# Six small loads for two, in a decode kernel bound by its transfers

## The chip, the cores and the metric

The kernel runs on one core of a Trainium2 chip. The metric is the device time of one execution, in microseconds; the median of several runs counts. The profile shows one execution, with times counted from the start of its span.

## The reference

The result is `x + attention(xn) + gMLP(xn)`, with `xn` the layer norm of `x`, for one decode step: four batch rows of 640 numbers, in bf16.

```python
# attention: 32 heads of 128, 4096 cached positions per batch row and head
q = (xn @ wq) -> [B, 32, 1, 128]
scores = einsum('bhqd,bhkd->bhqk', q, k_cache) * 128 ** -0.5
o = einsum('bhqk,bhkd->bhqd', softmax(scores), v_cache)
attention = o.reshape(B, 1, 4096) @ wo
# gMLP: w_in [640, 1728], w_out [864, 640]; the sequence has length 1
z = gelu(xn @ w_in);  z1, z2 = z[..., :864], layernorm(z[..., 864:])
gMLP = (z1 * (w_sp * z2 + b_sp)) @ w_out
```

The two caches are 134 MB each and every number of them is used once, so the work is mostly the reading of 282 MB.

## The kernel before

The caches are read in 16 runs (`NT`), one for each group of eight heads and each batch row: 8.4 MB of K and 8.4 MB of V per run. All of K, V and the early weights pass through one large SBUF tile, `ring`, which is cut into five units; K takes two units at a time and V one or two. For each quarter of a K run, DVE multiplies by the query (L555), often adds the halves (L575), PE sums (L584) and DVE finishes the row sums (L598). The softmax follows on DVE, ACT and PE, and PE multiplies the dealt-out probabilities with V (L657). At the end of a head group the output projection adds into `out_ps` (L755).

All loads but three tiny ones are issued by SyncE (SP), in an order written out by hand: a list `loads` of planned transfers, from which `pump()` sends the next one once the units that it overwrites were used. The first entries are: wq (L110, sent before the list), the first K run in two halves (L153), the gMLP's weights (`load_w`), the second K run (L153, one transfer of 8.4 MB), the first part of wo (L172), and the first run's V in two halves (L161). The second K run overwrites wq, so it must also wait for the last matmul of L357. The second V half overwrites the gMLP's weights, and so waits for the gMLP's last matmul (L516). ACT issues x (L96) and two scalars (L114, L115) at the very start.

`load_w` sends `w_in` (L133, 2160 KB), the first 768 rows of `w_out` (L134, 960 KB), and the last 96 rows of `w_out` in two transfers of 60 KB (L141). These 96 rows go to 16 + 16 partitions, three rows (`TR`) of 640 numbers to each, dealt so that neighbouring partitions hold rows from four different places (`NW`); a memset on GpSimd (L138) zeroes the partitions around them first.

The framework gives the transfers issued by SP and ACT eight semaphores, numbered 0 to 7, in turn, in the order of the program. A transfer that takes a semaphore again first waits, in its issuer's queue, until the transfer that had it before, eight earlier, has landed. In the order of the program the first eight are x (0), wq (1), the two scalars (2 and 3), the two halves of the first K run (4 and 5), `w_in` (6) and the large part of `w_out` (7). The two transfers of L141 then take 0 and 1, the second K run 2, wo 3, and so on. The last two of the program are the stores of the result: half of it from SP (L849), half from ACT (L851), on semaphores 2 and 3.

The program ends (L877) with five wait instructions on SP, each for two semaphores, a drain, and two barriers of all engines. The five wait for semaphores 3 and 2, 4 and 1, 5 and 0, then 6 and DVE, 7 and ACT, in this order.

Of the kernel before, what the change touches and what calls it, by code (L numbers as in the profile page):

```python
# [20 lines left out]
def kernel(  # L21
# [14 lines left out]
    nc = tc.nc  # L36
    P = nc.NUM_PARTITIONS
    Bsz, Sq, D = A_x.shape
# [20 lines left out]
    CW = 32  # L59
# [4 lines left out]
    NFF = Fh // P  # L64
    NW = 4
    TL = P // CG // 2
    TR = (Fh - NFF * P) // (2 * TL)
# [57 lines left out]
    w_out_sb = w_sb[:, DC * F : DC * F + NFC * D].rearrange("p (k n) -> p k n", k=NFC)  # L125
# [6 lines left out]
    def load_w():  # L132
        nc.sync.dma_start(out=w_in_sb, in_=B_w_in.rearrange("(p c) n -> p c n", c=DC))  # L133
        nc.sync.dma_start(  # L134
            out=w_out_sb[:, 0:NFF, :],
            in_=B_w_out[0 : NFF * P].rearrange("(p k) n -> p k n", k=NFF),
        )
        nc.gpsimd.memset(w_out_sb[:TN, NFF:, :], 0.0)  # L138
        for g in range(2):
            at = NFF * P + g * TL * TR  # L140
            nc.sync.dma_start(  # L141
                out=w_out_sb[g * CW : g * CW + TL, NFF:, :].rearrange("p r n -> p (r n)"),
                in_=B_w_out[at : at + TL * TR].rearrange("(k e r) n -> e k (r n)", e=NW, r=TR),
            )

    k_tiles, v_tiles = {}, {}
    V_CUTS = (0, UC // 2, 3 * UC // 4, 7 * UC // 8, UC)
# [45 lines left out]

    plan_k(0)
    plan("w", W_UNIT, 1, load_w)
    plan_k(1)
    plan_wo(0)
# [20 lines left out]
    def pump():  # L218
        while loads:
# [29 lines left out]
        out=lane_diag[:],  # L249
        in_=ident_f[:].rearrange("p (h l) -> p l h", h=HT),  # L250
# [5 lines left out]
        out=hmask[:],  # L256
        in_=ident_f[:].rearrange("p (h l) -> p h l", h=HT),
# [5 lines left out]
        out=head_scale[:].rearrange("p (h l) -> p h l", h=HT),  # L263
# [11 lines left out]
        out=sel[:],  # L275
        in_=ident_f[:].rearrange("p (g h k) -> p k h g", g=CG, k=GC),
# [5 lines left out]
        out=spread[:],  # L282
        in_=ident[:].rearrange("p (m r) -> p r m", r=HT)[:, :, None, :].to_broadcast(
            [P, HT, HT, LN]
        ),
# [3 lines left out]
        out=q_lanes[:].rearrange("r b (h l) -> r b h l", h=HT),  # L289
        in_=ident[: HT * Bsz, : HT * Bsz]  # L290
# [9 lines left out]
    for g in range(CG):  # L300
        ps = slice(g * QW, (g + 1) * QW)
        for hh in range(QH):
            at_col = (g % 2 * QH + hh) * Bsz
            nc.gpsimd.tensor_copy(
                out=place[ps, hh, at_col : at_col + Bsz], in_=lane_diag[ps, 0:Bsz]
# [13 lines left out]
    for i in range(NSTAT):  # L319
# [5 lines left out]
        out=rstd[:], in_=mv[:, 1:2], func=ACT.Sqrt, bias=eps_tile[:Bsz], scale=1.0  # L325
# [4 lines left out]
        out=xn_bf[:],  # L330
# [9 lines left out]
    for c in range(DC):  # L340
        nc.tensor.transpose(  # L341
            out=xnT_ps[:, c, :], in_=xn_v[:, c, :], identity=ident[:Bsz, :Bsz]
# [11 lines left out]
    for c in range(DC):  # L354
        for hg in range(NQG):
            g = hg % CG
            nc.tensor.matmul(  # L357
                out=q_ps[hg // CG][g * QW : (g + 1) * QW, :],
# [11 lines left out]
    def out_sum(half):  # L370
        return out_ps[OG * half : OG * half + Bsz, :]

    for half in range(2):
        nc.tensor.matmul(
            out=out_sum(half),
# [390 lines left out]
    with tc.manual_schedule(engines={E.PE, E.DVE, E.Activation, E.SP}):  # L766
# [80 lines left out]
        r0, r1 = slice(0, Bsz), slice(OG, OG + Bsz)  # L847
# [34 lines left out]
```

## Time and profile before

| | |
|---|---|
| median of three runs | 661.8 us (661.74 to 661.94) |
| the profiled execution: time, span | 661.8 us, 660.0 us |
| busy: PE, DVE, ACT | 324.5, 463.6, 84.9 us |
| DMA read, mean rate over the span | 282.24 MB, 428 GB/s |
| granted TensorE clock | 0.717 |
| chain that ended last: DMA, DVE, PE | 63%, 29%, 6% |
| landing of ACT's store, SP's last drain starts, end of span | 658.93, 659.26, 660.0 us |

The span covers the engines' instructions; 1.8 us of the execution lie around it. The chain is followed back from the last instruction: at each step to whatever released it. A transfer's landing is the last of the semaphore writes of the DMA engines that carry it, and "us to landing" counts from the start of its issue on the queue of SP or ACT. Beside the page and its views, the text uses the trace's single DMA packets (start, duration, size) and the single semaphore writes.

### The profile page before, as it was taken

To read this page: it belongs to the slowest core of one execution; us is meant where nothing else is said; L and a number is where in the kernel's file an instruction comes from. 1 tells how busy PE (TensorE), PEld (TensorE's weight loads), DVE (VectorE), ACT (ScalarE), POOL (GpSimd) and SP (SyncE) were. 2 spreads that over 40 slices of the span, in tenths; PEclk is the share of its full clock that TensorE was granted. 3 is DMA by queue.
4 is the path that set the end of the run, shared out by engine and by line. 5 is a ranking of instruction groups with operands and counts; after the bars stand their busy time and mean duration, and the time that the engine had idled before them with its cause. 6 is when DMAs were issued, how large, how long until landed. Compare 5 with 4: busy or idle time off the path is not lost.

```text
span 660.0 us, 4943 instructions
## 1 busy us (share of the span) xinstructions
PE 324.5 (49%) x2127; PEld 147.6 (22%) x2127; DVE 463.6 (70%) x268; ACT 84.9 (13%) x208; POOL 8.6 (1%) x31
## 2 busy tenths in 40 slices
PE   0257463625636463464625346253564525347756
PEld 0114131211312221131212123011231212213333
DVE  2497966939598694957949297692957849498840
ACT  0023011020200202020020200202020020201100
POOL 4000000000000000000000000000000000000000
PEclk9767585775857577686768878567786768887786
DMA  9999999999999999999999999999999999999997
GB/s 380 433 449 406 440 447 433 442 418 441 438 425 437 442 425 426 433 442 437 437 442 405 438 441 433 442 425 438 425 437 442 437 429 438 417 426 437 424 429 289
DMA packets 7977, 282.56 MB, mean 428 GB/s; under 512 B 872, under 2 KB 2036, under 8 KB 2452
## 3 DMA queue, kind: packets, MB, share of 16 engines
q1 hardware_dynamic: 7936, 282.24, 99.1%
q8 instruction: 16, 0.26, 0.1%
q14 instruction: 5, 0.04, 0.0%
q10 hardware_dynamic: 20, 0.01, 0.0%
HBM read 282.24 MB, written 0.01 MB: 428 GB/s over the span
## 4 chain that ended last, share of the span: by engine, by line
DMA 63%; DVE 29%; PE 6%; issue 1%; ACT 0%; SPq 0%; DVEq 0%
DMA ring<-in_A_k_cache_dram 53%; DVE ring L555 20%; DMA ring<-in_A_v_cache_dram 9%; DVE halved L575 5%; PE s_ps L584 3%; DVE ring L575 3%; PE pv_acc L657 1%; PE zT L416 1%; DVE s_sb L598 0%; PE out_ps L755 0%; ACT L471 0%; PE pv L675 0%; SPq L161 0%; PE pv L687 0%; DVE o_r L743 0%
## 5 line engine op out<-in xcount | busy, mean ns | idle before, releaser
L555 DVE TENSOR_TENSOR ring<-ring,qbc 128x8192 bf16<-128x8192 bf16 x64 | 282.0, 4418 | 90.5 <-DMA ring<-in_A_k_cache_dram 90.5
L584 PE MATMUL s_ps<-ring,ident 128*128 128x512 bf16 x480 | 169.0, 521 | 259.6 <-DVE ring L575 152.2
L584 PEld LDWEIGHTS <-ident 128*128 128x128 bf16 x608 | 73.6, 121 | 409.6 <-issue 289.5
L575 DVE TENSOR_TENSOR ring<-ring 128x4096 bf16<-128x4096 bf16 x36 | 82.5, 2291 | 1.2
L657 PE MATMUL pv_acc<-ring,pm 128*32 128x512 bf16 x1008 | 73.0, 433 | 6.1 <-DMA ring<-in_A_v_cache_dram 6.1
L598 DVE TENSOR_REDUCE s_sb<-s_ps 128x64 f32<-128x512 f32 x64 | 43.9, 685 | 24.1 <-PE s_ps L584 24.0
L671 ACT COPY pv_sb<-pv_acc 128x512 f32<-128x512 f32 x16 | 9.4, 586 | 392.1 <-PE pv_acc L657 392.1
L584 PE MATMUL s_ps<-halved,ident 128*128 128x512 bf16 x128 | 39.9, 468 | 31.2 <-DVE halved L575 31.2
L632 ACT ACTIVATE pm<-p,hmask 128x256 bf16<-128x256 bf16 x120 | 49.5, 494 | 0.5
L657 PEld LDWEIGHTS <-pm 128*32 128x32 bf16 x1008 | 39.4, 145 | 41.1 <-issue 31.6
L575 DVE TENSOR_TENSOR halved<-ring 128x4096 bf16<-128x4096 bf16 x16 | 36.6, 2290 | 0.5
L617 DVE TENSOR_REDUCE nb<-max_ps 128x1 f32<-128x16 f32 x16 | 2.8, 174 | 38.1 <-PE max_ps L611 38.1
L675 PE MATMUL pv<-sel,pv_sb 128*128 128x8 f32 x128 | 17.0, 259 | 11.2 <-ACT pv_sb L671 11.2
L675 PEld LDWEIGHTS pv<-sel,pv_sb 128*128 128x128 f32 x128 | 15.5, 191 | 18.8 <-ACT pv_sb L671 18.8
L716 DVE TENSOR_TENSOR o_n<-pv,rden 128x32 bf16<-128x32 f32 x4 | 0.8, 191 | 14.4 <-PE pv L687 14.3
L609 ACT ACTIVATE lay<-lane_diag,m 128x16 f32<-128x16 f32 x16 | 4.9, 309 | 45.6 <-DVE m L607 45.6
L621 ACT ACTIVATE p<-s_sb,nb 128x256 bf16<-128x256 f32 x16 | 8.1, 508 | 20.6 <-DVE nb L617 20.6
L699 POOL TENSOR_TENSOR own_sum<-acc,hmask 128x32 f32<-128x32 f32 x4 | 2.0, 500 | 618.0 <-ACT p L621 618.0
L541 ACT CAST q_rows<-qr_ps 32x128 bf16<-32x128 f32 x4 | 1.0, 255 | 55.2 <-PE qr_ps L533 55.2
L611 PE MATMUL max_ps<-lay,head_scale 128*128 128x16 f32 x32 | 6.1, 265 | 3.1 <-ACT lay L609 3.1
L607 DVE TENSOR_REDUCE m<-s_sb 128x1 f32<-128x256 f32 x16 | 6.7, 420 | 0.5
L341 PE MATMUL xnT_ps<-ident,xn_bf 4*128 4x4 bf16 x5 | 0.4, 178 | 11.6 <-DVE xn_bf L329 11.6
(96 smaller groups left out, 88.4 us busy)
## 6 DMA issues: line engine op xcount, KB each, us to landing
ring<-in_A_v_cache_dram SPq DMA_DIRECT2D x7, 4096.0 KB, 21.9
ring<-in_A_k_cache_dram SPq DMA_DIRECT2D x2, 4096.0 KB, 29.2
ring<-in_A_wq_dram SPq DMA_DIRECT2D x1, 5120.0 KB
wo<-in_A_wo_dram SPq DMA_DIRECT2D x3, 1280.0 KB, 17.1
ring<-in_B_w_in_dram SPq DMA_DIRECT2D x1, 2160.0 KB, 38.5
ring<-in_A_v_cache_dram SPq DMA_DIRECT2D x1, 2048.0 KB, 20.5
ring<-in_A_v_cache_dram SPq DMA_DIRECT2D x1, 1024.0 KB
ring<-in_A_v_cache_dram SPq DMA_DIRECT2D x2, 512.0 KB
```

The costliest lines, as they stand in the source:

```text
L416: nc.tensor.matmul(out=zT[: P if k < NFF else TN, t, k, :], lhsT=w_t[:, 2 * c + t, k, :] if k < NFF else w_edge[:, 2 * c + t, k - NFF, :], ...
L555: nc.vector.tensor_tensor(out=t, in0=t, in1=qbcs[i // Bsz][:, i % Bsz, None, :].to_broadcast([P, QC, Dh]), op=ALU.mult,)
L575: nc.vector.tensor_tensor(out=h[:, :, 0:HD2], in0=t[:, :, 0:HD2], in1=t[:, :, HD2:Dh], op=ALU.add)
L584: nc.tensor.matmul(out=s[:], lhsT=ident[:], rhs=t[:, :, g * RW : (g + 1) * RW], start=(g == 0), stop=(g == n - 1),)
L598: nc.vector.tensor_reduce(out=scores[i][:, q * QC : (q + 1) * QC], in_=sums_ps.pop((i, q))[:], axis=AX.X, op=ALU.add,)
L607: nc.vector.tensor_reduce(out=m1[:], in_=scores[i][:], axis=AX.X, op=ALU.max)
L611: nc.tensor.matmul(out=ps[:], lhsT=head_scale[:], rhs=d[:], start=True, stop=True)
L621: nc.scalar.activation(out=p[:], in_=scores.pop(i)[:], func=ACT.Exp, bias=nb[:], scale=scale_qk, accum_out=acc[hg % NACC][:, b : b + 1],)
L632: nc.scalar.activation(out=p_m[i % 2][:, :, h, :], in_=probs[i][:].rearrange("p (n c) -> p n c", c=BC), func=ACT.Copy, scale=hmask[:, h : ...
L657: nc.tensor.matmul(out=pv_acc[g * CW : (g + 1) * CW, :], lhsT=pm[:, n, :, :].rearrange("p h (k c) -> p c (h k)", k=GC)[:, c, :], rhs=v_nat ...
L671: nc.scalar.copy(out=pv_sb[:], in_=pv_acc[:])
L675: nc.tensor.matmul(out=pvs[hg][:, :, b], lhsT=pv_sb[:, k * Dh : (k + 1) * Dh], rhs=sel[:, k, :], start=(k == 0), stop=stop and k == GC - 1,)
```

## The change

The first of the two small transfers becomes four, of four partitions each (every fourth partition of the 16, one contiguous 3,840-byte run to each). The second becomes two, by columns: the first two of the three rows of each partition, then the third. The bytes, their places and the zeroing are the same. Since six transfers stand where two stood, every later transfer takes a semaphore four further on: the second K run takes 6, wo 7, and the stores of the result 6 and 7. In the changed file all later lines move down by six: L153 becomes L159, L161 L167, L172 L178, L849 L855, L851 L857 and L877 L883.

```diff
         for g in range(2):
             at = NFF * P + g * TL * TR
-            nc.sync.dma_start(
-                out=w_out_sb[g * CW : g * CW + TL, NFF:, :].rearrange("p r n -> p (r n)"),
-                in_=B_w_out[at : at + TL * TR].rearrange("(k e r) n -> e k (r n)", e=NW, r=TR),
-            )
+            src = B_w_out[at : at + TL * TR].rearrange("(k e r) n -> e k (r n)", e=NW, r=TR)
+            dst = w_out_sb[:, NFF:, :].rearrange("p r n -> p (r n)")
+            lanes = slice(g * CW, g * CW + TL)
+            if g == 0:
+                for k in range(TL // NW):
+                    nc.sync.dma_start(out=dst[g * CW + k : g * CW + TL : NW], in_=src[:, k])
+            else:
+                for r0, r1 in ((0, TR - 1), (TR - 1, TR)):
+                    cs = slice(r0 * D, r1 * D)
+                    nc.sync.dma_start(out=dst[lanes, cs], in_=src[:, :, cs])
```

## The prediction

> **What bounds the kernel now.** I read the page first (engine shares, the 40 slices, the DMA queues), then the chain that ended last, then SP's timeline at the start, the rows of the lines that issue the weights, and last the trace's single DMA packets.
>
> From the page:
>
> ```profile
> PE 324.5 (49%) x2127; PEld 147.6 (22%) x2127; DVE 463.6 (70%) x268; ACT 84.9 (13%) x208; POOL 8.6 (1%) x31
> DMA  9999999999999999999999999999999999999997
> ...
> q1 hardware_dynamic: 7936, 282.24, 99.1%
> q8 instruction: 16, 0.26, 0.1%
> ```
>
> Queue q1 (everything that SP issues) keeps the 16 DMA engines busy for 99.1% of the span; no compute engine passes 70%. The kernel is bound by its transfers, so a microsecond in which DMA engines stand still is lost for good, and a late compute step costs nothing while transfers are queued. The chain of waits, around the second K run:
>
> ```profile
> 74.19 2.30 DVE halved L575
> 76.51 0.04 issue
> 76.55 28.43 DMA ring<-in_A_k_cache_dram
> ```
>
> The chain passes through DVE and SP's issue, but this load of 8.39 MB takes 28.4 us where its bytes need 19.3 at the packets' pace (below): it stands some 9 us behind earlier transfers. DVE or SP may come that much later before an engine runs dry. SP's own timeline at the start:
>
> ```profile
> 1.18 0.94 SPq L153 DMA_DIRECT2D ring<-in_A_k_cache_dram  x2
> 2.15 0.98 SPq L133 DMA_DIRECT2D ring<-in_B_w_in_dram  x1
> 3.17 0.53 SPq L134 DMA_DIRECT2D ring<-in_B_w_out_dram  x1
> 3.82 12.95 SPq L141 DMA_DIRECT2D ring<-in_B_w_out_dram  x2
> 20.27 0.34 SPq L153 DMA_DIRECT2D ring<-in_A_k_cache_dram  x1
> 20.65 0.42 SPq L172 DMA_DIRECT2D wo<-in_A_wo_dram  x1
> 39.34 26.87 SPq L161 DMA_DIRECT2D ring<-in_A_v_cache_dram  x2
> ```
>
> The second K run goes out at 20.27, released by L357's last matmul, 20 us before the engines reach it. The packets show the rest: each DMA engine works off its share in the order of issue, back to back (65,536 bytes every 2.415 us). On eleven engines the second K run's first packet starts at 41.48 to 41.92, straight behind w_out's last; on five, held up by L141 or a late start, at 42.56 to 42.97. Eight of the eleven are each interrupted twice by the page's 16 "instruction" packets (q8, 16 KB of code each), at 1.42 us a time: the packet itself 0.88 to 0.99, and the next K or V packet 2.89 to 2.97 instead of 2.42 (the excess is smaller on packets of half that size). These eight, whose second K run began at 41.48 to 41.79, are with one other the last to end: their last wo pieces land at 656.4 to 656.7, the other seven engines' at 653.9 to 655.7. The end is set by those eight.
>
> **The change, part by part.** The profiled execution took 661.8 us, 660.0 of them span, and 661.8 is also the median of the runs, so sums on its span apply to the median as they stand.
>
> *The tail.* SP ends with five wait instructions for two semaphores each and a drain:
>
> ```profile
> L877 SPq EVENT_SEMAPHORE  x7: 17/28/28, 658.9 to 659.9; - x7
> ```
>
> The first two-semaphore wait holds the stores' two (2 and 3). It passes at 658.944, after ACT's store lands at 658.93; four waits on things long done follow at 659.009, .070, .134 and .196, the drain at .261. With the stores on 6 and 7, three of the waits pass while the stores fly, the fourth at SP's store (landed 658.75), the fifth at 658.944, and the drain comes at about 659.01. Four steps of 0.063 go: **-0.25 us**. Nothing stands against it: the barriers behind the drain wait for SP.
>
> *The bytes.* On the engines, each L141 is 4 packets of 3,840 bytes, 149 ns each, on four engines. After: four transfers of one such packet on four engines, then the second group in packets of 2,560 and 1,280, by bytes some 99 and 50 ns. Per engine 8 x 149 = 1.19 us stays, plus four more closing semaphore packets of 9 ns: +0.04. The four engines are not among the eight; the nearest one ends 0.28 us before the last. Cost nothing; without that cover, 0.04. The Trainium skill, "DMA: Bandwidth & Descriptors", Rules for kernel authors, speaks against the split: coalesce small transfers, since under 64 KB one mostly pays overhead; here the second L141 lands 0.60 us behind the first on each engine, which is its 4 x 149 ns and no fixed part, so the trace does not agree for transfers queued behind others.
>
> *SP's issues.* L141 takes SP 0.80 and 0.64. Four more, at most 3.2 us, fall between 16 and 36 while SP has nothing else to send. PE's matmuls with the last weights must wait for six semaphores instead of two, at some 0.06 each 0.25 us later; behind them is L161's second V half (65.88), which stands behind queued work until 73.5. Nothing.
>
> *Who waits for whom at the start.* A DMA waits until the one eight issues before it, on the same semaphore, has landed. The six small ones now follow x, wq, the two scalars and the first K run's halves, which land by 35.5. But the second K run's predecessor moves from a scalar (landed 7.8) to **w_in**, and the wo load's from the other scalar to w_out. After these the spacing is eight as before, so only the names change. w_in lands late:
>
> ```profile
> L133 SPq DMA_DIRECT2D ring<-in_B_w_in_dram x1: 976/976/976, 2.2 to 2.2; - x1
> ...
> DMA to landing us min/median/max: 38.5/38.5/38.5
> ```
>
> 2.155 + 38.5 = 40.62, by its slowest engine (the others' shares land at 39.4 to 40.0). So the second K run is issued at 40.62 + 0.08 (a semaphore wait and the step behind it on SP) = 40.70 instead of 20.27. Behind it in SP's queue are wo (w_out lands 42.9) and the first V half, 39.34 before, about 43.4 after; both have the second K run's 19.3 us of packets as cover. Nothing for these two.
>
> *From issue to first packet.* No transfer of before is issued to engines about to run dry, except the very first: L110, issued at 0.734, has its first packets at 1.74 to 1.90 on twelve engines (1.01 to 1.16 later), on the other four at 2.08 to 2.80. So the second K run starts at 41.71 to 41.86. Engines that were to begin at 41.48 to 41.68 run dry. A stream that restarts is slow in its first packet: after a code load by 0.47 to 0.55 us, in L110's by 0.64 to 1.19 on most engines. I take 0.5, from the code load, since it is the row on a running machine with packets of this size. The eight engines then run as if begun at about 42.3, where the last of them had begun at 41.79: **+0.5 us** at the end. Bounds: none lost, if packets come at once; or L110's slowest engine, whose first packet ended at 5.20, as if begun at 3.68, 2.95 after issue: 40.70 + 2.95 - 41.79 = +1.9. The Trainium skill has in the same page, Latency and other measured facts, about 600 ns to the first byte of a DMA issued by SP; by that the packets would come at 41.30 and nothing would run dry, which is the first rival.
>
> Sum: 661.8 - 0.25 + 0.5 = **662.0 us**. K's own later landing (62.97 before; DVE takes it at 63.06) pushes DVE by the same half microsecond and then the next K issue from 76.55, covered by 9 us.
>
> **The rivals.**
> - *No gap*: the packets come before 41.48. For it: SP's 0.38 us of issuing is part of the 1.01 I counted, and the first transfer was cold. Against: the two stores at the end take 0.83 and 0.88 from issue to first packet too. It leaves the tail: 661.55. Chance 0.2.
> - *A cold restart, slower than before*: eleven engines restart together, as in L110, and one of the eight starts like L110's slowest: +1.9 - 0.25 = 663.4. For it: the only start from nothing in this trace. Against: that was one engine of sixteen. It is slower by over 0.2% once an engine of the eight counts as begun after 41.79 + 1.3 + 0.25 = 43.35. Chance 0.13; restarts between, at 662.4 to 662.9, are my forecast's upper side.
> - *A fixed cost per small transfer on its engines*, as large as SP's 0.80 for issuing: 4 x 0.80 - 0.28 - 0.25 = +2.7, 664.5. The 0.60 between the two L141 speaks against. Chance 0.02.
> - *The change does not do what it says*: the stores sit on other semaphores. The built program has them on 6 and 7; left out. Faster by over 0.2% needs more than the whole tail step; one code load less on each of the eight would spare 1.42 and give 660.1, but the change leaves PE's code as long as it was. Chance 0.03 for it and the like.
>
> **How the numbers follow.** The forecast, 661.8 to 662.9 with the restart at about half a microsecond, has 0.62. A measurement of this kernel tells about 0.2%, 1.3 us, from no change: forecast and first rival lie within, so same 0.82; slower 0.15 from the second and third; faster 0.03. The range takes in the first rival and most of the way to the second: 661.4 to 663.1.
>
> **What would show it.** In the profile after: SP's second K issue (L159) at 40.7 and wo behind 42.9; DMA packets of the second K run starting at 41.7 to 41.9 with first packets near 2.9 us; the last wo landing 0.5 later against the span's start; SP's last drain 0.07 after the store's landing instead of 0.32. Wrong, if L159 goes out near 20, if the first packets join w_out's without a gap, or if the eight engines no longer end last.

## The result, and the profile after

| | before | after |
|---|---|---|
| median of the runs side by side, us | 661.96 (661.74 to 662.16) | 663.78 (663.16 to 664.40) |
| ratio | | 1.0027, 95% interval 1.0017 to 1.0036 |
| profiled execution: time, span, us | 661.8, 660.0 | 663.82, 662.0 |
| second K run issued | 20.27 | 40.73 |
| second K run landed | 62.97 | 65.46 |
| last wo piece landed | 656.67 | 658.66 |
| ACT's half of the result cast | 657.17 | 659.30 |
| last store landed, SP's last drain | 658.93, 659.26 | 661.12, 661.26 |

The change costs 1.8 us; 662.0 was forecast. The page of after, for the same lines as before:

```profile
PE 319.6 (48%) x2127; PEld 148.8 (22%) x2127; DVE 463.5 (70%) x268; ACT 84.9 (13%) x208; POOL 8.7 (1%) x31
...
DMA  9999999999999999999999999999999999999997
GB/s 376 434 400 421 438 439 432 444 432 440 433 424 428 444 436 437 424 433 440 436 425 440 437 424 440 429 440 441 420 436 437 432 436 437 432 411 438 437 419 280
...
q1 hardware_dynamic: 7968, 282.25, 99.0%
q8 instruction: 16, 0.26, 0.1%
```

The same rates line on the page of before:

```profile
GB/s 380 433 449 406 440 447 433 442 418 441 438 425 437 442 425 426 433 442 437 437 442 405 438 441 433 442 425 438 425 437 442 437 429 438 417 426 437 424 429 289
```

The busy shares tell nothing: a DMA engine counts as busy while a slow packet runs. The rates do. By the end of the fourth slice before has moved (380 + 433 + 449 + 406) x 16.50 us = 27.5 MB, after (376 + 434 + 400 + 421) x 16.55 us = 27.0 MB in 0.2 us more: 0.62 MB short, 1.4 us at 428 GB/s (roughly, since the line counts a whole packet in the slice where it starts). The loss arises in the third slice, 33 to 50 us: 400 where before has 449. The chain there:

```profile
2.65 38.01 DMA ring<-in_B_w_in_dram
40.66 0.02 issue
40.68 0.02 SPq L159
40.70 0.03 issue
40.73 24.73 DMA ring<-in_A_k_cache_dram
65.46 0.03 issue
65.49 0.02 DVEq L561
65.51 0.04 issue
65.56 4.43 DVE ring L561
```

No part of the chain of before is a wait for `w_in`; now its landing releases SP (L159), and the second K run takes 24.73 us from its issue. SP's timeline:

```profile
0.73 0.38 SPq L110 DMA_DIRECT2D ring<-in_A_wq_dram  x1
1.18 1.43 SPq L159 DMA_DIRECT2D ring<-in_A_k_cache_dram  x2
2.65 0.52 SPq L133 DMA_DIRECT2D ring<-in_B_w_in_dram  x1
3.22 0.53 SPq L134 DMA_DIRECT2D ring<-in_B_w_out_dram  x1
3.86 14.14 SPq L146 DMA_DIRECT2D ring<-in_B_w_out_dram  x4
25.83 10.30 SPq L150 DMA_DIRECT2D ring<-in_B_w_out_dram  x2
40.73 0.34 SPq L159 DMA_DIRECT2D ring<-in_A_k_cache_dram  x1
42.97 0.33 SPq L178 DMA_DIRECT2D wo<-in_A_wo_dram  x1
43.41 1.48 SPq L167 DMA_DIRECT2D ring<-in_A_v_cache_dram  x1
```

The K issue stands at 40.73 where it stood at 20.27, wo at 42.97. The single packets show the rest. A DMA engine is called dry here while it has no packet to work on. On the engine that finishes first, the last packet of `w_out` ends at 41.44. The second K run's first packets start at 41.69 to 42.50 on ten engines and take 2.67 to 3.50 us (2.418 before, on all sixteen); on two others they start at 43.54 and 44.41 and take 3.21 and 3.81; the other four start at 42.65 to 43.02 and take 2.42 to 2.75. Second packets take up to 2.76. Nothing is made up later: the last V halves' closing packets come at 641.76 to 645.15 against 640.36 to 643.19, 1.40 later for the first of them and 1.96 for the last, and the last wo piece lands 1.99 later.

The end of the program:

```profile
L883 SPq EVENT_SEMAPHORE  x7: 17/28/28, 660.1 to 661.9; - x7
L883 SPq DRAIN  x3: 7/7/7, 661.3 to 661.6; - x3
```

The first of the waits now starts at 660.1, a microsecond before the last store lands at 661.12, and the drain starts 0.14 behind that landing instead of 0.33: 0.19 saved. (Last to land is ACT's store in before and SP's in the change.) But ACT's cast follows the last wo piece by 0.64 instead of 0.50, and the store lands 1.82 behind the cast's start instead of 1.76. So 1.99 + 0.14 + 0.06 - 0.19 = 2.00, the difference of the drains and of the spans.

### The profile page after: what moved, and what is told of

The parts are those of the page before. It is cut to its first block, busy times and chain, and to the rows that moved or that the text cites. A ratio compares the mean times of both kernels' runs of the same rounds, so it can differ in the third digit from the quotient of the medians.

```text
span 662.0 us, 4953 instructions
## 1 busy us (share of the span) xinstructions
PE 319.6 (48%) x2127; PEld 148.8 (22%) x2127; DVE 463.5 (70%) x268; ACT 84.9 (13%) x208; POOL 8.7 (1%) x31
## 4 chain that ended last, share of the span: by engine, by line
DMA 66%; DVE 28%; PE 5%; issue 0%; SPq 0%; ACT 0%; DVEq 0%; ACTq 0%
DMA ring<-in_A_k_cache_dram 57%; DVE ring L561 20%; DMA ring<-in_B_w_in_dram 6%; DVE halved L581 5%; DMA ring<-in_A_v_cache_dram 3%; PE s_ps L590 3%; DVE ring L581 2%; PE pv_acc L663 1%; PE pv L681 0%; DVE s_sb L604 0%; PE out_ps L761 0%; PE pv L693 0%; SPq L159 0%; ACT pv_sb L677 0%; DVE res L854 0%
## 5 line engine op out<-in xcount | busy, mean ns | idle before, releaser
L590 PE MATMUL s_ps<-ring,ident 128*128 128x512 bf16 x480 | 164.3, 509 | 262.4 <-DVE ring L581 155.5
L663 PE MATMUL pv_acc<-ring,pm 128*32 128x512 bf16 x1008 | 69.9, 418 | 7.2 <-DMA ring<-in_A_v_cache_dram 7.2
L604 DVE TENSOR_REDUCE s_sb<-s_ps 128x64 f32<-128x512 f32 x64 | 43.9, 685 | 23.2 <-PE s_ps L590 23.2
L590 PE MATMUL s_ps<-halved,ident 128*128 128x512 bf16 x128 | 41.4, 482 | 34.9 <-DVE halved L581 34.9
L681 PE MATMUL pv<-sel,pv_sb 128*128 128x8 f32 x128 | 18.6, 272 | 11.1 <-ACT pv_sb L677 11.1
L681 PEld LDWEIGHTS pv<-sel,pv_sb 128*128 128x128 f32 x128 | 17.1, 208 | 19.2 <-ACT pv_sb L677 19.2
```

The costliest lines, as they stand in the source:

```text
L590: nc.tensor.matmul(out=s[:], lhsT=ident[:], rhs=t[:, :, g * RW : (g + 1) * RW], start=(g == 0), stop=(g == n - 1),)
L604: nc.vector.tensor_reduce(out=scores[i][:, q * QC : (q + 1) * QC], in_=sums_ps.pop((i, q))[:], axis=AX.X, op=ALU.add,)
L663: nc.tensor.matmul(out=pv_acc[g * CW : (g + 1) * CW, :], lhsT=pm[:, n, :, :].rearrange("p h (k c) -> p c (h k)", k=GC)[:, c, :], rhs=v_nat ...
L681: nc.tensor.matmul(out=pvs[hg][:, :, b], lhsT=pv_sb[:, k * Dh : (k + 1) * Dh], rhs=sel[:, k, :], start=(k == 0), stop=stop and k == GC - 1,)
```

## The experiments

The theory after the result: the second K run is issued too late for the DMA engines, and loses more than the prediction allowed. Rivals: the small transfers themselves cost engine time; GpSimd's memset L407, which now waits for four of them (it runs at 43.05, and ACT's copies of L412 at 44.4 instead of 40.7), makes the gMLP late; or a share of each K packet is lost, not a fixed time. In the table "ahead" is the time from the second K run's issue to the point where the first engine has nothing else left, in the profiled execution; below zero the engines were dry already when it was issued (for the last three rows from before's 41.5). "Median" is over all executions of a run, and "beside before" is against the median of before measured with it.

| run | K issued | ahead | its first packets, us | median | beside before |
|---|---|---|---|---|---|
| before | 20.27 | 21 | 2.42 | | |
| five small | 35.43 | 5.9 | 2.42 | 661.63 | -0.3 |
| w_out first | 37.97 | 3.4 | 2.42 | 661.88 | 0.0 |
| lead 2.8 | 38.20 | 3.2 | 2.42 | 662.17 | +0.3 |
| lead 2.2 | 39.00 | 2.4 | 2.42 to 3.03 | 662.45 | +0.6 |
| lead 1.6 | 39.61 | 1.8 | 2.46 to 4.02 | 663.59 | +1.7 |
| wo between | 42.84 | 1.6 | 2.48 to 3.43 | 663.54 | +1.6 |
| lead 1.0 | 40.00 | 1.4 | 2.54 to 4.05 | 663.67 | +1.8 |
| K run in halves | 40.48 | 0.8 | 1.21 to 2.46 (half the size) | 663.88 | +2.0 |
| the change | 40.73 | 0.7 | 2.42 to 3.81 | 663.78 | +1.8 |
| four pads | 40.66 | 0.7 | 2.42 to 3.34 | 663.91 | +2.0 |
| w_out in halves | 41.77 | -0.3 | 2.78 to 3.36 | 663.89 | +2.0 |
| seven small | 42.91 | -1.4 | 2.66 to 3.53 | 665.08 | +3.2 |
| nine small | 44.10 | -2.6 | 2.42 to 3.79 | 666.83 | +4.9 |

**`w_out` ahead of `w_in`**, so that the same six small transfers stay and the K run waits for the smaller load:

```diff
-        nc.sync.dma_start(out=w_in_sb, in_=B_w_in.rearrange("(p c) n -> p c n", c=DC))
         nc.sync.dma_start(
             out=w_out_sb[:, 0:NFF, :],
             in_=B_w_out[0 : NFF * P].rearrange("(p k) n -> p k n", k=NFF),
         )
+        nc.sync.dma_start(out=w_in_sb, in_=B_w_in.rearrange("(p c) n -> p c n", c=DC))
```

> The changed kernel with the order of w_in and the large part of w_out exchanged, so that the second K run waits for w_out, which now lands first. Theory (the second K run is issued too late and the DMA engines run dry): it is issued at about 37.8 us, while w_in still has 4 us to go, its first packets join w_in's or the small ones' without a gap and take 2.42 us; the loss is gone and the tail's gain remains, 661.7 us. Rival (the six small transfers cost their engines time): they are all still there, 663.8 us. Rival (GpSimd's memset L407 now waits for four of the small transfers, and with it the gMLP's first steps come 3.7 us later): it still waits until 43, 663.8 us.

Measured 661.88 against 661.92, ratio 0.9999 (0.9990 to 1.0008). SP's timeline:

```profile
37.97 0.34 SPq L159 DMA_DIRECT2D ring<-in_A_k_cache_dram  x1
43.05 0.33 SPq L178 DMA_DIRECT2D wo<-in_A_wo_dram  x1
43.49 0.37 SPq L167 DMA_DIRECT2D ring<-in_A_v_cache_dram  x1
```

Only the K issue has moved against the change, from 40.73 to 37.97; wo and V go out where the change sends them. The loss is gone. All six small transfers and the late memset are still there, so both of these rivals fall. The rates line says the same:

```profile
GB/s 380 437 445 406 442 445 433 442 429 425 442 425 437 438 429 434 425 438 445 429 446 417 426 441 437 438 425 438 433 429 442 433 433 438 421 422 439 426 426 288
```

Its third slice holds 445 (449 before, 400 in the change).

**Before, with four loads of 256 bytes a row added** behind the two small ones: the turn of the semaphores alone.

```diff
+        pad0 = edge0 + DC * 2 * TR * TN
+        for j in range(4):
+            cs = slice(pad0 + j * P, pad0 + (j + 1) * P)
+            nc.sync.dma_start(out=w_sb[0:NW, cs], in_=B_w_out[NW * j : NW * (j + 1), 0:P])
```

> The kernel before, with its two small transfers whole, and four loads of 4 x 256 bytes into unused places behind them: the semaphores turn by four as in the change, without splitting anything and without the memset's wait. Theory of the dry engines: the second K run waits for w_in again and is issued at 40.7, the first packets take 2.7 to 3.8 us, and the time is that of the change, 663.8 us. Rival of the small transfers' cost: four more transfers, but of 256-byte packets, at most 0.1 us of bytes; between 661.7 and 663.8. Rival of the memset: it is back at 3 us, so 661.7 us.

Measured 663.91, ratio 1.0029 (1.0018 to 1.0039): the change's loss without its split, and with GpSimd's memset back at 3.24. **Five, seven and nine small transfers** move the second K run's predecessor: with five it is the second half of the first K run, with seven `w_out`, with nine one of the small ones.

```diff
-                for r0, r1 in ((0, TR - 1), (TR - 1, TR)):
+                for r0, r1 in ((0, TR),):                        # five
+                for r0, r1 in ((0, 1), (1, 2), (2, TR)):         # seven
+                for c0 in range(0, TR * D, TR * P):              # nine, cs = slice(c0, c0 + TR * P)
```

> Five small transfers instead of six: the first in four as in the change, the second whole. The second K run then waits for the second half of the first K run, which lands at 35.5, and the stores take semaphores 5 and 6. Theory of the dry engines: issued at 35.6, no gap, 661.96 less three steps of 0.063 in the tail, 661.8 us. Rival of the small transfers' cost: three quarters of the loss of the change, 663.2 us. Rival of the memset: it waits as in the change, 663.8 us.

> Seven small transfers: the second in three parts, by rows. The second K run then waits for w_out, which lands last of the large weights at 42.95. Theory of the dry engines: issued at 43.0, 2.3 us later than in the change, and every microsecond of it is lost: 666.1 us, the first packets again 2.7 to 3.8 us long. Rival of the small transfers' cost: five quarters of the loss, 664.3 us. Rival of the memset: 663.8 us.

> Nine small transfers, the second in five parts by columns: the last of them wait for w_out and for the first small one, each takes SP 0.65 us to issue, and the second K run goes out at about 44.3 us, 1.4 after that of seven small ones. The engines are all empty by then, so that the whole 1.4 is lost: 666.5 us. If only 0.6 of each further microsecond is lost, as between the change and seven: 665.9 us.

Measured 661.63 (ratio 0.9999, 0.9990 to 1.0007), 665.08 (1.0048, 1.0036 to 1.0061) and 666.83 (1.0072, 1.0059 to 1.0085). One transfer fewer and the loss is gone; with seven and nine all engines stand empty and it grows. The account is plain there: with seven the engines are dry from about 41.5 to 43.9, and the first packets take about 3.2 instead of 2.4: 2.4 + 0.8 = 3.2, as measured (my 666.1 for seven put too much on the restart). With nine it is 41.5 to 45.1 and more, and again 0.8: at least 4.4, measured 4.9.

**The second K run in two transfers of 4.2 MB**, whose packets are half as large:

```diff
-        step = (1 if i == 0 else 2) * UNIT
+        step = (1 if i < 2 else 2) * UNIT
```

> The changed kernel with the second K run in two transfers of 4096 KB, issued at 40.7 and behind w_out at 42.9: packets of 32 KB instead of 64 at the restart. If a restart costs an engine a fixed time: the first packets take 1.21 plus the same 0.25 to 1.1 us, 663.8 us as in the change. If what is lost is a share of the first packet's time: half of it, 663.0 us.

Measured 663.88, ratio 1.0029 (1.0017 to 1.0041). The first packets take up to 2.14 where 1.213 is normal, an excess of up to 0.9, and 2.46 on one straggler that starts at 44.22; on packets of twice the size the change has up to 1.1, and 1.4 on its last straggler. The time is that of the change, where half the excess would have given 663.0. So what is lost is a time and not a share of the first packet, and this rival falls.

**`w_out` in two halves**, the K run waiting for the first:

```diff
-        nc.sync.dma_start(
-            out=w_out_sb[:, 0:NFF, :],
-            in_=B_w_out[0 : NFF * P].rearrange("(p k) n -> p k n", k=NFF),
-        )
+        for k0, k1 in ((0, NFF // 2), (NFF // 2, NFF)):
+            nc.sync.dma_start(
+                out=w_out_sb[:, k0:k1, :],
+                in_=B_w_out[0 : NFF * P].rearrange("(p k) n -> p k n", k=NFF)[:, k0:k1, :],
+            )
```

> The changed kernel with the large part of w_out in two halves of 480 KB, so that the second K run waits for the first of them: issued at about 41.9 us, between the change (40.7) and seven small ones (42.9). If a restart costs the same each time and every further microsecond of emptiness is lost in full: seven's time less 1.0, 664.0 us. If an incomplete stop (some engines still at work) costs more per engine, as the change's first packets of 2.7 to 3.8 us and its slow second packets suggest beside seven's 2.7 to 3.5: 664.4 to 664.9 us.

Measured 663.89, ratio 1.0029 (1.0017 to 1.0040). Most engines are dry from 41.5 to 42.75, then 0.8 in the first packets: 2.05, measured 1.96. This K run was issued a microsecond later than the change's and costs hardly more: the restart here is even (all sixteen first packets start between 42.73 and 43.60), while the change has two stragglers.

**The first wo load moved ahead of the small ones**: 1.3 MB more stand before the K run, so that the engines have work until after its first packets come.

```diff
             in_=B_w_out[0 : NFF * P].rearrange("(p k) n -> p k n", k=NFF),
         )
+        load_wo(0)
...
     plan_k(1)
-    plan_wo(0)
```

> The changed kernel with the first wo load (1280 KB, 3.05 us of the engines) moved ahead of the small transfers. The second K run then waits for w_out and is issued as late as with seven small ones, at 43.0 us, but the engines have wo to work on until 44.5. Theory of the dry engines: no gap, first packets of 2.42 us, 661.8 us. Rival (it is the lateness of the second K run, or of the gMLP's first steps behind GpSimd's memset, that costs, whatever the engines do): 665 us as with seven.

This was the surprise. Measured 663.54, ratio 1.0024 (1.0015 to 1.0034), not 661.8. The chain:

```profile
3.18 39.60 DMA ring<-in_B_w_out_dram
42.78 0.02 issue
42.80 0.02 SPq L160
42.81 0.03 issue
42.84 24.40 DMA ring<-in_A_k_cache_dram
67.24 0.03 issue
```

Issued at 42.84, the K run has its first packets from 44.48 on. On fourteen engines they follow straight behind the packet before them; two engines stand dry first, until 45.01 and 46.83. Yet the first packets take up to 3.43, on an engine without a gap, and the run lands at 67.24, where 62.97 of before and wo's 3.05 us ahead of it would make 66.0. My theory that engines lose only what they stand still, plus a restart, falls with it: packets that follow without a gap, 1.6 us after the issue of their transfer, are slow as well.

**So the lead itself was varied.** `w_in` is cut by columns, its second part sent behind `w_out`; the K run waits for `w_out`, and the second part is the work that the engines have in hand. Only `cut` differs: 3968, 2944, 1936 and 944 of 8640 columns.

```diff
-        nc.sync.dma_start(out=w_in_sb, in_=B_w_in.rearrange("(p c) n -> p c n", c=DC))
+        w_in_flat = w_sb[:, 0 : DC * F]
+        B_w_in_flat = B_w_in.rearrange("(p c) n -> p (c n)", c=DC)
+        cut = 2944
+        nc.sync.dma_start(out=w_in_flat[:, :cut], in_=B_w_in_flat[:, :cut])
         nc.sync.dma_start(
             out=w_out_sb[:, 0:NFF, :],
             in_=B_w_out[0 : NFF * P].rearrange("(p k) n -> p k n", k=NFF),
         )
+        nc.sync.dma_start(out=w_in_flat[:, cut:], in_=B_w_in_flat[:, cut:])
```

> w_in is split by columns around w_out, so that the second K run waits for w_out and 1168 KB of w_in (2.8 us of the engines) stand between w_out's landing and the engines' need of it: issued some 1.0 us ahead, no gap. If a fixed 3.3 us must pass from the issue to the full rate (by the run with wo moved ahead, slowest of the eight), 3.3 - 1.0 = 2.3 us are lost: 664.0. If instead a transfer that comes too late loses one amount however late it is, 1.7 us: 663.5. If only a gap costs, nothing: 661.8.

> As before it, with 1424 KB of w_in behind w_out: issued some 1.6 us ahead, as in the run with wo moved ahead. Fixed time of 3.3 us: 1.7 us lost, 663.4. One amount: 663.5. Only a gap costs: 661.8.

> With 1676 KB of w_in behind w_out: issued some 2.2 us ahead. Fixed time of 3.3 us: 1.1 us lost, 662.8. One amount: 663.5, or 661.8 if 2.2 us are ahead enough. Only a gap costs: 661.8.

> With 1924 KB of w_in behind w_out: issued some 2.8 us ahead. Fixed time of 3.3 us: 0.5 us lost, 662.3. One amount: 663.5, or 661.8 if 2.8 us are ahead enough. Only a gap costs: 661.8.

Measured against 661.85: 663.67 (ratio 1.0029, 1.0019 to 1.0039), 663.59 (1.0025, 1.0016 to 1.0034), 662.45 (1.0008, 0.9999 to 1.0017), 662.17 (1.0005, 0.9996 to 1.0014). `w_out` landed earlier than I had reckoned, so the leads were 1.4, 1.8, 2.4 and 3.2. On SP wo and V go out when they did (of the rest, only the last small transfer moves with `cut`); the second run, then the third:

```profile
39.61 0.35 SPq L163 DMA_DIRECT2D ring<-in_A_k_cache_dram  x1
42.94 0.33 SPq L182 DMA_DIRECT2D wo<-in_A_wo_dram  x1
```

```profile
39.00 0.34 SPq L163 DMA_DIRECT2D ring<-in_A_k_cache_dram  x1
42.96 0.33 SPq L182 DMA_DIRECT2D wo<-in_A_wo_dram  x1
```

Issuing the one load 0.6 us earlier is worth 1.1 us. In the packets: at a lead of 1.8 the first ones take 2.53 to 4.02 on fifteen engines (2.46 on the last to start, at 44.23); twelve of the sixteen follow without a gap, and these take up to 3.94. At 2.4 all but two take 2.42 to 2.47, and these two 3.02 and 3.03, 0.6 too long (one other engine stands dry for 0.7 first); at 3.2 all sixteen take 2.418 and the span is 659.8. "Only a gap costs" falls at a lead of 1.8 (at 1.4 several engines did run dry, so that run doesn't decide it). It is the lead that counts and not the hour of the issue: wo between, issued 3.2 us after the run with a lead of 1.8, loses about the same.

A profile shows one execution, and these differ: the one with a lead of 3.2 (661.60) is among the fastest of its run, 661.52 to 662.73, the one with 1.8 (664.21) the slowest of 661.85 to 664.21, and wo's (662.96) the fastest of 662.96 to 664.01. So the packets of these three are not those of a median execution, and a lead of 3.2 may not be free in each.

The other two theories both fit the four runs within their intervals: with the measured leads, a fixed 3.3 us from issue to full rate would give losses of 1.9, 1.5, 0.9 and 0.1, and one amount until enough is ahead gives 1.7, 1.7 and then less; measured 1.8, 1.7, 0.6 and 0.3. But the fixed time fails further down the table, where the loss stays at 1.6 to 2.0 from a lead of 1.8 down to -0.3 (it would ask for 3.6 at the end of that). What is left is the account by engines: the time for which one stands dry, plus the excess of its first packets. Where all stop alike, the sums above bear it out (2.05 against 1.96, 3.2 against 3.2, 4.4 against 4.9). Where they restart unevenly it is argued and not shown, since the packets on record don't name their engine and the one that ends last can't be followed from 42 to 656. Without a gap the excess is uneven and reaches 1.5 (3.94 against 2.42); behind a long gap it is more even, about 0.8; that the two nearly make up for each other in between is a reading of the table's plateau.

Not settled: why first packets are slow, and why some engines' far more than others', in the same transfer. No record shows what an engine does inside a packet.

## Why the prediction was wrong

*What bounds the kernel*: right. What the engines lost at 42 us was still missing at 656, with no compute engine in between giving any of it back. Whether the same eight engines end last was not followed.

*Who waits for whom*: right within 0.07 us: the K issue at 40.70 forecast, 40.73 measured; wo behind 42.9, measured 42.97; the first V half about 43.4, measured 43.41. Neither of these two cost anything: the run with `w_out` first has them at the same times, without loss.

*The bytes, and SP's issues*: right. With the six transfers kept and the K run earlier, 661.88 against 661.92. The rule on coalescing that the prediction cites from the Trainium skill, "DMA: Bandwidth & Descriptors", Rules for kernel authors, would have made the split itself the cost; the run with `w_out` first and the one with five small ones show that it is not, for transfers queued behind others.

*The tail*: the waits behave as forecast, 0.19 of the 0.25; the missing step of 0.06 is there because SP's store, which the fourth wait holds, now lands last. The gain does not reach the time: the casts and the stores took 0.20 longer in the profiled execution of the change. That they did so too where nothing is late (with `w_out` first, 0.64 from the last wo piece to the cast and 1.83 from there to the landing) shows that the restart is not its cause; the cause was not followed up. The granted clock between 648 and 652 us was 0.89 in the profile of before and 0.50 in these two.

*From issue to first packet*: this step failed, by its second half. The first packets were forecast at 41.71 to 41.86, and from 41.69 they came, though ten engines' spread to 42.50 and two came at 43.54 and 44.41. (By the Trainium skill's figure of about 600 ns to the first byte, "DMA: Bandwidth & Descriptors", Latency and other measured facts, they would have come at 41.3, an estimate, without a gap; the trace has 0.96 and more. The prediction's 0.83 and 0.88 for the two stores at the end are 0.77 and 0.79 in the trace, which changes nothing. And a stream without a gap would not have helped: with none on fourteen engines, the run with wo between lost 1.6.) The mis-sized term is the restart, +0.5 taken from the packets behind a code load; measured, gap and slow packets together, +1.4 on the first engine to end its V and +1.96 on the last. The code load's row was chosen as the one on a running machine with packets of this size, but there only one engine is interrupted, with its next packets long since issued. The other row, L110's own start (a first packet that ends as if begun up to 2.95 after issue), was the transfer that is short of lead, as here; its slowest engine gave +1.9, and the prediction set it aside as one engine of sixteen. With several engines of uneven restart, and the end set by the last of them, the slowest is the one to count. That rival's 663.4, given a chance of 0.13, stands 0.4 from the result, most of it the tail that did not come through; that its +1.9 comes so near to +1.96 is in part luck, as engines and executions differ by more.

Also wrong was the thought behind "no gap": that a transfer which arrives just in time costs nothing. Of the other rivals, the fixed cost of small transfers is refuted above.

## What to carry to other kernels

When a kernel's time is its transfers, ask of every large load not only whether it is issued before the engines run dry, but how long before: here it had to be about 3 us, and 1.8 us ahead, with an unbroken stream of packets on most engines, lost about as much as 0.7. Adding or splitting transfers shifts which earlier transfer each later one must wait for; look the new predecessor up for every load behind the edit, and if it lands late, exchange the order of two early loads (here `w_out` ahead of `w_in`), which took the whole loss away. No version here beats the kernel before by more than the measurement tells.

## What the hardware showed unexpectedly

A load of 8.4 MB over sixteen engines ran all its first packets at full pace (2.418 us for 65,536 bytes) only when it was issued some 3 us ahead; from 1.8 us downwards they took up to 4.05 behind a gap, and up to 3.94 without one. The loss did not shrink with the packet: 2.0 us with packets of 32,768 bytes, whose excess reached 0.9, and 1.2 on one engine. The engines of one transfer restart unevenly: in the change two began 1.0 and 1.9 us behind the ten others' last.
